# All expert weights resident in SBUF and read through registers, and scan runs of 128 steps, in a gated scan followed by a top-1 mixture of experts

## The chip, the core and the metric

The kernel runs on one core of a Trainium2 chip. The metric is the device time of one execution in microseconds (us), lower is better. Five engines work side by side on a core: PE (TensorE, matrix products; the profile counts its weight loads apart as PEld), DVE (VectorE), ACT (ScalarE), POOL (GpSimd) and SP (SyncE, which here issues most DMAs). Each engine has a sequencer that reads its instructions in order; register and address instructions run on the sequencer itself, and the profile marks these with a q (PEldq, SPq).

## The reference

A gated linear recurrence over time, and then for each token one expert of eight, chosen by a router.

```python
B, S, D = 4, 5056, 256            # x, r_gate, i_gate: (B, S, D)
N, E, F = 20224, 8, 1024          # w1: (E, D, F), w2: (E, F, D)
a_t = exp(8 * sigmoid(r_gate) * log(clip(sigmoid(a_param), 1e-6, 1 - 1e-6)))
xg = sqrt(max(1 - a_t * a_t, 1e-6)) * sigmoid(i_gate) * x
h = 0
for t in range(S):                # for each batch row and channel
    h = a_t[:, t] * h + xg[:, t]
    y[:, t] = h
x2 = y.reshape(N, D)
logits = x2 @ w_gate + modality_bias[modality_id]
e_idx = argmax(logits, axis=1)
gate = softmax(logits)[arange(N), e_idx]
for e in range(E):                # each token by its own expert only
    m = e_idx == e
    out[m] = gate[m, None] * (maximum(x2[m] @ w1[e], 0) @ w2[e])
```

All of it is float32. The kernel keeps that precision with numbers split in two fp16 parts (high and low): each product of the expert layers is three fp16 products, high by high, high by low and low by high.

## The kernel before

**The scan.** Time is cut into runs (`CHUNKS`): 19 runs of 256 steps, one of 128 and one of 64. A run takes all 4 batch rows, so 256 steps are 1024 tokens. `load_chunk` loads its three inputs by DMAs that SP issues (L467), `scan_chunk` makes the factors on ACT and DVE and scans on DVE (L518), `split_chunk` finds a scale (L606) and writes the two fp16 parts (L627 on ACT, L630 on DVE), `route_chunk` computes router and slot numbers, and `rows_part` turns the states into rows of tokens (DMA transposes, L669) and scatters them with POOL (L777) into a table `rows` in DRAM, which holds each expert's tokens in one place, in order of arrival. Every run costs the same number of small DVE instructions, whatever its length.

**The experts' weights.** The experts are put in an order by their router bias. Of each, w1 and w2 are loaded (1 MB each), scaled by a power of two, and split into two fp16 parts (`convert`). The parts of w2 stay in SBUF, in `w2f`. The parts of w1 are written to DRAM, into `w1s`.

**Pages.** The expert layers work on pages of 256 tokens (or 128; a few of 512, as two halves) of one expert. `choose_pages` picks, on DVE, the expert with the most tokens waiting; expert and place in the table are known only as numbers in a tile `sel`, so the program reads them into registers (`value_load`). For each page, SP (`page_weights`, L949 to L959) loads the w1 parts of the page's expert from `w1s` into one of three buffers `wt` (1 MB per page, L953), and `load_rows` the tokens, transposed, into `X` (L990).

**The expert layers** (`expert_layers`) are a pipeline on PE: layer 1 of a page in four quarters (L1065), each followed by a quarter of layer 2 of the page before (L1108). A quarter of layer 1 is 12 pairs of a weight load and a matmul: the stationary operand is a 128x128 block of w1, the streamed operand `X`, as many columns as the page has tokens. A quarter of layer 2 is 12 pairs for 256 tokens and 6 for 128: the stationary operand is a block of `H`, the streamed one 256 columns of w2. Layer 1's `wt` is a fixed address, since the page's weights were copied there. Layer 2 reads `w2f` at a place that depends on the page's expert, in a register:

```python
(wv[:, s, k, fs], cur.X[:, 2 * x + k, :])                              # layer 1: stationary, streamed
(prev.H[:, hx, f, rs_], w2f[:, ds(pg.ew + (f * 2 + wx) * D, D)])       # layer 2: stationary, streamed
```

The register is loaded once per page (L1088); each use of `ds(pg.ew + ...)` costs an address instruction on the sequencer of PE. Behind layer 1, ACT and DVE write the two parts of `H` (L1009, L1011); behind layer 2, ACT scales the output (L1020) and POOL scatters it (L1024).

**The order of the work** is fixed when the program is built: a planner (`run`) keeps a list of threads, each a generator that asks for an engine, a duration and a condition, and emits next the one that can start first. `START` lists the order of the first loads by hand. The first 28 pages may be "early": of an expert among those whose weights are ready, the first two experts at least, and of 128 tokens where fewer than 511 wait. The last pages are of 128 tokens; five of them stand in branches that run only where tokens are left, and none of the five ran in the profiled execution (PE read the register of 84 pages).

Of the kernel before, what the change touches and what calls it, by code (L numbers as in the profile page):

```python
# [9 lines left out]
F32 = mybir.dt.float32  # L10
F16 = mybir.dt.float16
# [17 lines left out]
CHUNKS = [(0, 256), (256, 256)] + [(512 + 256 * k, 256) for k in range(17)] + [(4864, 128), (4992, 64)]  # L29
BUFS = {  # L30
    "a": 3, "g": 2, "x": 2, "wt": 3, "H": 2, "X": 3, "ot": 3, "rt": 2, "sel": 4, "dg": 2,
# [5 lines left out]
TAIL_TAGS = "aaggxxa"  # L37
# [35 lines left out]
def kernel(  # L73
# [27 lines left out]
    w1s = dram.tile([E, P, 4 * FF], F16, name="w1s")  # L101

# [45 lines left out]
    for e in range(E):  # L148
        nc.gpsimd.memset(tieb8[:, e : e + 1], 0.125 * (E - 1 - e))
        nc.gpsimd.memset(kd[:, e : e + 1], float(E - 1 - e - 8 * e * NCAP))  # L150
    cpar = const.tile([P, 2], F32, name="cpar")
# [15 lines left out]
    nc.vector.tensor_reduce(out=top[:, :, 0], in_=mb[0:1], axis=AX.X, op=ALU.max)  # L167
    nc.vector.tensor_tensor(out=low, in0=mb[0:1], in1=top.broadcast_to([1, 2, E]), op=ALU.subtract)
# [21 lines left out]
    # half of 8 * log(clip(sigmoid(a_param)))  # L190
# [49 lines left out]
    def add(gen, prio, t=0.0, urgent=False):  # L240
        """prio: the lower the sooner, (on TensorE, on the other engines)"""
# [30 lines left out]
    WE = NF * 2 * D  # L272
    w2f = const.tile([P, E * WE + WE // 2], F16, name="w2f")
    w2r = w2f[:, 0 : E * WE].rearrange("p (e f s d) -> p e f s d", e=E, f=NF, s=2)

    def waiting(q):
        """where a matrix waits, as it came: from the middle of one place to that of the next"""
        return w2f[:, q * WE + WE // 2 : (q + 1) * WE + WE // 2].bitcast(F32)

    READY = "pages read the weights of experts that are ready"  # L280

    def weight_write(ins, q, what="w"):
        """a write of which the pages of before read nothing"""
        tc.declare_no_dep(ins, group=f"{what}_pages", reason=READY)
        tc.add_to_no_dep_group(f"{what}{q}", ins)

    def weight_read(ins, pg, what="w"):
        for q in range(pg.ready, E):
            tc.declare_no_dep(ins, group=f"{what}{q}", reason=READY)
# [13 lines left out]
    def scale_of(name, raw, sc, iv, factor):  # L303
        """sc: the power of two for a matrix, iv: what undoes it"""
        ss = sm.tile([P, 1], F32, name=f"ss{name}", tag="ss", bufs=16)
# [3 lines left out]
        pt = pso.tile([P, 512], F32, name=f"pt{name}", tag="po")  # L309
        # the upper halves of the words are the values as bf16: enough for a power of two  # L310
# [5 lines left out]
        jk = sm.tile([P, P], F32, name=f"jk{name}", tag="jk", bufs=1)  # L316
# [9 lines left out]
    ivc = const.tile([P, E], F32, name="ivc")  # L326

    def convert(k, name, raw, hi, lo, sc, q=None):
        """hi = sc * raw, rounded; lo = sc * raw - hi, by VectorE or by TensorE and ScalarE; a half at a time"""
        wrote = lambda ins: None if q is None else weight_write(ins.ins, q)  # L330
        if LO[k] == "P":
            yield "ACT", 0.2, room("dg")
            td = take("dg")
            dg = sm.tile([P, P], F32, name=f"dg{name}", tag="dg")
            nc.scalar.activation(dg, ident, AF.Copy, scale=sc)
        for v in range(2):
            fs = slice(4 * v, 4 * v + 4)
            if HI[k] == "A":
                yield "ACT", 1.0, None
                wrote(nc.scalar.activation(hi[:, fs, :], raw[:, fs, :], AF.Copy, scale=sc))  # L340
            else:
                yield "DVE", 0.63, None
                wrote(nc.vector.tensor_scalar(out=hi[:, fs, :], in0=raw[:, fs, :], scalar1=sc, scalar2=None, op0=ALU.mult))
            if LO[k] == "D":
                yield "DVE", 1.2, None
                wrote(nc.vector.scalar_tensor_tensor(
                    out=lo[:, fs, :], in0=raw[:, fs, :], scalar=sc, in1=hi[:, fs, :], op0=ALU.mult, op1=ALU.subtract
                ))
                continue
            for u in range(2):  # L350
                yield "PE", 1.25, room("ph"), 0.2
                tp = take("ph")
                us = slice(4 * v + 2 * u, 4 * v + 2 * u + 2)
                pl = psh.tile([P, 2, 256], F32, name=f"pl{name}_{v}{u}", tag="ph")
                nc.tensor.matmul(pl, dg, raw[:, us, :], start=True, stop=False)
                nc.tensor.matmul(pl, nid, hi[:, us, :], start=False, stop=True)
                yield "ACT", 0.48, None, -0.5
                wrote(nc.scalar.activation(lo[:, us, :], pl, AF.Copy))  # L358
                give("ph", tp)
        if LO[k] == "P":  # L360
            give("dg", td)

    # the loads before the expert layers start have a fixed order
    loads, seq = [], {"a": 0, "b": 0}
    for what in START.split():
        if what in seq:
            seq[what] += 1
            what += str(seq[what] - 1)
        loads.append(what)
    assert seq == {"a": E, "b": E}  # L370
    assert all(loads.index(f"a{e}") < loads.index(f"b{e}") for e in range(E // 2, E))
# [6 lines left out]
    def place(e):  # L378
        """the place in w2f where w1 waits"""
        return e + E // 2 if e < E // 2 else e  # L380

    def first_weights(e):
        """w1 of the e-th expert in the order, left in DRAM as its two parts"""
        tag = "wt"
        q = place(e)
        yield "DMA", 2.9, seen(("turn", loads.index(f"a{e}") - 1), *([("w1", e - E // 2)] if e >= E // 2 else [])), -9.0
        raw = waiting(q)
        o = nc.sync.value_load(order[0:1, e : e + 1], min_val=0, max_val=E - 1)
        weight_write(nc.sync.dma_start(
            raw.rearrange("p (k f) -> p k f", k=2), w1[ds(o, 1)].rearrange("o (k p) f -> p (o k) f", p=P)  # L390
        ).ins, q)
        went(f"a{e}")
        mark["got", 1, e] = plan["end"]
        yield "SP", 0.0, seen(("got", 1, e)), 0.0
        sc = sm.tile([P, 1], F32, name=f"sc1_{e}", tag="sc1", bufs=8)
        yield from scale_of(f"1_{e}", raw, sc, ivc[:, e : e + 1], 1.0)
        yield "SP", 0.0, room(tag), 0.0
        tw = take(tag)
        wt = pm.tile([P, 4 * FF], F16, name=f"wk{e}", tag=tag, bufs=BUFS[tag])
# [810 lines left out]
```

## Time and profile before

| what | value |
|---|---|
| time, median of 3 runs | 1205.32 us (1198.14 to 1214.27) |
| span of the profiled execution, first to last instruction | 1136.6 us |
| own time of the profiled execution | not given apart from its span; the median of the runs is 68.7 us above the span |
| PE busy | 949.4 us (84%) |
| DVE, ACT, POOL busy | 768.2 (68%), 588.2 (52%), 455.1 (40%) us |
| moved by DMA | 268.3 MB, 236 GB/s |
| mean granted clock of TensorE | 0.936 |

The span is what the profile can divide; what lies around it, 68.7 us, is taken as a constant. In the rows of the profile, "L1108" is line 1108 of the kernel, `po<-w2f,H` says what is written from what, and "x3840" is a count. A matmul's duration in the rows is from its start to its modelled end; matmuls overlap, so the pace of a row of them is told by the distance of their starts.

### The profile page before, as it was taken

The page shows a single profiled execution, that of the slowest core. Times are in us where ns is not written, and L with a number is a line of the kernel's source. Part 1 is how long each engine was busy: PE and PEld are TensorE (multiplying, and loading weights), DVE is VectorE, ACT ScalarE, POOL GpSimd, SP SyncE. Part 2 cuts the span into 40 slices and gives each one's busy share as a digit, 9 for nine tenths or more (in the row PEclk, how much of TensorE's full clock was granted, in tenths as well). Part 3 has the DMA queues.
Part 4 walks back from the last instruction along what each step waited for, and adds up shares of the span by engine and source line. Part 5 has one row for each costly group of instructions (what it writes and reads, how often), then busy time and mean ns, then how long its engine had stood idle before and what let it go on. Part 6 is the DMA issues. An engine that isn't in the chain of part 4 may idle for free.

```text
span 1136.6 us, 29582 instructions
## 1 busy us (share of the span) xinstructions
PE 949.4 (84%) x9139; PEld 818.5 (72%) x9139; DVE 768.2 (68%) x2544; ACT 588.2 (52%) x824; POOL 455.1 (40%) x496
## 2 busy tenths in 40 slices
PE   1423996898894998985999899999999999999993
PEld 1211875777783887874788678777778888889993
DVE  2896783778793978876787778687876433344561
ACT  4752752673743466666367566765754333333331
POOL 3026131615440626546544655375646311242121
PEclk9756998999996999998999999999999999999997
DMA  7799999999999999997999999999978635559999
GB/s 258 313 256 193 237 225 223 306 257 317 263 255 194 201 229 320 259 249 191 253 271 255 294 282 276 220 289 268 277 173 202 144 85 163 150 161 241 243 265 186
DMA packets 257752, 268.30 MB, mean 236 GB/s; under 512 B 216319, under 2 KB 224640, under 8 KB 237888
## 3 DMA queue, kind: packets, MB, share of 16 engines
q1 hardware_dynamic: 238848, 214.82, 77.6%
q0 software_dynamic: 15744, 42.92, 13.1%
q10 hardware_dynamic: 3008, 8.57, 2.3%
q8 instruction: 89, 1.46, 0.5%
q14 instruction: 63, 0.52, 0.2%
HBM read 172.62 MB, written 51.56 MB: 197 GB/s over the span
## 4 chain that ended last, share of the span: by engine, by line
PE 47%; DMA 20%; DVE 18%; issue 5%; SPq 4%; ACT 4%; POOL 1%; ACTq 0%; DVEq 0%; POOLq 0%
PE ph L1065 23%; PE po L1108 22%; DMA X<-rows 6%; DMA w2f<-in_moe_w_dram 6%; DVE g L518 4%; DVE H L1011 3%; DMA rows<-rt,di 2%; DVE mxy L606 2%; DVE g L504 1%; DMA iv<-iv 1%; SPq L669 1%; DVE a L630 1%; PE pt L314 1%; ACT H L1009 1%; DMA x<-in_x_dram 1%
## 5 line engine op out<-in xcount | busy, mean ns | idle before, releaser
L1065 PE MATMUL ph<-X,wt 128*128 128x256 f16 (+1 forms) x4224 | 491.8, 268 | 47.4 <-DMA X<-rows 46.0
L1108 PE MATMUL po<-w2f,H 128*128 x3840 | 486.9, 274 | 10.4 <-issue 7.4
L1065 PEld LDWEIGHTS <-wt 128*128 128x128 f16 x4224 | 390.2, 100 | 99.0 <-issue 51.0
L1108 PEld LDWEIGHTS <-H 128*128 128x128 f16 x3840 | 372.7, 98 | 61.8 <-issue 9.0
L1009 ACT ACTIVATE H<-ph 128x512 f16<-128x512 f32 (+1 forms) x352 | 195.1, 555 | 367.4 <-PE ph L1065 357.0
L1011 DVE SCALAR_TENSOR_TENSOR H<-ph,H 128x512 f16<-128x512 f32 (+1 forms) x352 | 222.1, 636 | 235.3 <-ACT H L1009 234.6
L1024 POOL DMA_INDIRECT out_dram<-ot,mt x160 | 200.1, 1251 | 405.9 <-ACT ot L1020 313.2
L777 POOL DMA_INDIRECT rows<-rt,di x158 | 213.3, 1350 | 246.2 <-DVE dmy L534 55.5
L1020 ACT ACTIVATE ot<-po,gt 128x256 f32<-128x256 f32 x160 | 75.4, 471 | 75.6 <-PE po L1108 69.2
L518 DVE TENSOR_TENSOR_SCAN g<-a,g 128x2048 f32<-128x2048 f32 (+2 forms) x21 | 87.5, 4168 | 0.6
L627 ACT ACTIVATE a<-g,scy 128x512 f16<-128x512 f32 (+2 forms) x84 | 53.5, 686 | 16.2 <-DVE scy L545 14.3
L630 DVE SCALAR_TENSOR_TENSOR a<-g,scy,a 128x512 f16<-128x512 f32 (+2 forms) x84 | 56.6, 711 | 0.2 <-ACT a L627 0.2
L314 PEld LDWEIGHTS <-w2f 128*128 128x128 bf16 x256 | 20.6, 118 | 43.7 <-DMA w2f<-in_moe_w_dram 42.1
L314 PE MATMUL pt<-w2f 128*128 128x128 bf16 x256 | 23.2, 259 | 33.2 <-DMA w2f<-in_moe_w_dram 32.7
L495 ACT ACTIVATE a<-a,ch 128x1024 f32<-128x1024 f32 (+2 forms) x42 | 48.9, 1186 | 3.3 <-DVE m1y L531 3.3
L504 DVE TENSOR_TENSOR g<-g,x 128x2048 f32<-128x2048 f32 (+2 forms) x21 | 45.4, 2160 | 7.7 <-ACT x L502 7.7
L486 ACT ACTIVATE g<-g 128x2048 f32<-128x2048 f32 (+2 forms) x21 | 38.0, 1808 | 17.8 <-DMA g<-in_i_gate_dram 17.7
L490 DVE SCALAR_TENSOR_TENSOR g<-g,x 128x2048 f32<-128x2048 f32 (+2 forms) x21 | 45.2, 2152 | 0.8 <-ACT g L486 0.6
L606 DVE TENSOR_REDUCE mxy<-g 128x4 bf16<-128x2048 f32 (+2 forms) x21 | 45.0, 2144 | 0.0
L498 ACT ACTIVATE x<-a 128x2048 f32<-128x2048 f32 (+2 forms) x21 | 38.0, 1809 | 3.0 <-issue 2.4
L502 ACT ACTIVATE x<-x 128x2048 f32<-128x2048 f32 (+2 forms) x21 | 38.0, 1809 | 0.4
L488 ACT ACTIVATE a<-a 128x2048 f32<-128x2048 f32 (+2 forms) x21 | 37.8, 1801 | 0.4 <-ACT wk L358 0.4
(161 smaller groups left out, 654.8 us busy)
## 6 DMA issues: line engine op xcount, KB each, us to landing
wt<-w1s SPq DMA_DIRECT2D x89, 1024.0 KB
a<-in_r_gate_dram SPq DMA_DIRECT2D x19, 1024.0 KB
g<-in_i_gate_dram SPq DMA_DIRECT2D x19, 1024.0 KB
x<-in_x_dram SPq DMA_DIRECT2D x19, 1024.0 KB
w2f<-in_moe_w_dram SPq DMA_DIRECT2D x16, 1024.0 KB
w1s<-wk ACTq DMA_DIRECT2D x8, 1024.0 KB
out_dram<-ot,mt POOLq DMA_INDIRECT x160
rows<-rt,di POOLq DMA_INDIRECT x158
```

What stands on the lines that cost most here:

```text
L314: nc.tensor.matmul(pt[:, 0:P], blk, blk, start=(j == 0), stop=(j == nb - 1))
L504: nc.vector.tensor_tensor(out=g, in0=g, in1=s, op=ALU.mult)
L518: nc.vector.tensor_tensor_scan(out=g, data0=a, data1=g, initial=0.0, op0=ALU.mult, op1=ALU.add)
L606: nc.vector.tensor_reduce(out=mx[:, 0:ng], in_=yg.rearrange("p h g t -> p g h t"), axis=AX.XY, op=ALU.max, apply_absolute_value=True)
L630: nc.vector.scalar_tensor_tensor(out=ys[:, 1, :, g, :], in0=yg[:, :, g, :], scalar=sc[:, g : g + 1], in1=ys[:, 0, :, g, :], op0=ALU.mult, ...
L777: ins = nc.gpsimd.indirect_dma_start(out=rows[:, :], out_offset=bass.IndirectOffsetOnAxis(ap=idx, axis=0), in_=src, in_offset=None, bounds ...
L1009: nc.scalar.activation(t.H[:, 0, hs, :], ph[:, :, 0:st], AF.Relu)
L1011: nc.vector.scalar_tensor_tensor(out=t.H[:, 1, hs, :], in0=ph[:, :, 0:st], scalar=0.0, in1=t.H[:, 0, hs, :], op0=ALU.max, op1=ALU.subtract,)
L1020: nc.scalar.activation(t.ot[:, a, :], po, AF.Copy, scale=t.gt[:, a : a + 1])
L1024: ins = nc.gpsimd.indirect_dma_start(out=out[:, :], out_offset=bass.IndirectOffsetOnAxis(ap=t.mt[:, a, 0:1], axis=0), in_=t.ot[:, a, :], i ...
L1065: nc.tensor.matmul(ph[:, v, 0:st], lhsT, rhs, start=(m == 0), stop=(m == len(mm) - 1))
L1108: ins = nc.tensor.matmul(po, lhsT, rhs, start=(f == 0 and m == 0), stop=(f == NF - 1 and m == len(mm) - 1))
```

## The change

- The split parts of w1 and w2 of all 8 experts stay in SBUF, in one tile `wall` (132 KB per partition). `w1s`, the buffers `wt` and the loads per page go away. `first_weights` and `second_weights` become one function, `weights`, and `page_weights` becomes `page_rows`, without the load of w1.
- Layer 1 takes its stationary blocks from `wall` at an address in a register. The register is loaded ahead of layer 1 (L1012) instead of layer 2.
- Runs of the scan: one of 64 steps and then 39 of 128. Rows go out in parts of 4 columns, not 8. The first loads (`START`) are run 0, run 1, four matrices, run 2, two matrices, and so on.
- The low parts of the weights are all made on DVE; before, four matrices went through PE and ACT. The output buffers hold 128 rows each, and the last pages' tokens lie in other buffers. Comments were taken out.

```diff
-CHUNKS = [(0, 256), (256, 256)] + [(512 + 256 * k, 256) for k in range(17)] + [(4864, 128), (4992, 64)]
+CHUNKS = [(0, 64)] + [(64 + 128 * k, 128) for k in range(39)]
...
-PART = 8
+PART = 4
...
-HI = "ADDADDADADAAADDD"
-LO = "PDDDDDDDDPPDPDDD"
-START = "0 a a a a 1 b 2 b 3 b a b 4 b 5 a b a b a b"
+HI = "ADADADADADADADAD"
+LO = "DDDDDDDDDDDDDDDD"
+START = "0 1 w w w w 2 w w 3 w w 4 w w 5 w w 6 w w w w"
...
-    WE = NF * 2 * D
-    w2f = const.tile([P, E * WE + WE // 2], F16, name="w2f")
+    WE = 4 * FF
+    wall = const.tile([P, 2 * E * WE + WE // 2], F16, name="wall")
...
-    def page_weights(pg):
+    def page_rows(pg):
...
-        yield "DMA", 2.9, allof(room(tag), seen(*[("w1s", e) for e in range(pg.ready)]))
+        yield "DMA", 0.1, seen(*[("e", e) for e in range(pg.ready)])
+        pg.off = nc.sync.value_load(pg.sel[0:1, 0:1], min_val=0, max_val=NULLS + 256 - pg.size)
...
-        pg.wt = (pm if tag == "wt" else pa).tile([P, 4 * FF], F16, name=f"wt{pg.n}", tag=tag, bufs=BUFS[tag])
-        weight_read(nc.sync.dma_start(pg.wt, w1s[ds(es, 1)].rearrange("o p f -> (o p) f")).ins, pg, "d")
...
+                        if pg.ew is None:
+                            pg.ew = nc.tensor.value_load(pg.sel[0:1, 2:3], min_val=0, max_val=(E - 1) * 2 * WE)
...
                         mm = [
-                            (wv[:, s, k, fs], cur.X[:, 2 * x + k, :])
+                            (wall[:, ds(pg.ew + (2 * k + s) * FF + f * P, P)], cur.X[:, 2 * x + k, :])
                             for k in range(2) for s, x in ((0, 0), (0, 1), (1, 0))
                         ]
...
-                            (prev.H[:, hx, f, rs_], w2f[:, ds(pg.ew + (f * 2 + wx) * D, D)])
+                            (prev.H[:, hx, f, rs_], wall[:, ds(pg.ew + WE + (f // 4 * 2 + wx) * FF + f % 4 * D, D)])
```

What the two programs hold, in the order in which an engine meets it (ISA is a register or address instruction; the names behind an instruction are what it writes and reads):

On PE, before the change, the end of a page's layer 1 and the first quarter of layer 2 of the page before:

```order
L1065 LDWEIGHTS wt_913
L1065 MATMUL ph_0_0_1039<-X_0_990,wt_913 128x256
L1088 TENSOR_LOAD sel_779
L1088 ISA x2
L1108 LDWEIGHTS H_0_934
L1108 ISA
L1108 MATMUL po_0_0_1080<-w2f,H_0_934 128x256
```

On PE after the change, at the same place of the first page:

```order
L1027 ISA
L1027 LDWEIGHTS wall
L1027 ISA
L1027 MATMUL ph_0_3_819<-X_0_725,wall 128x128
L1066 LDWEIGHTS H_0_761
L1066 ISA
L1066 MATMUL po_0_0_841<-wall,H_0_761 128x256
```

A pair of layer 1 had no address instruction and now has two, one ahead of the weight load and one ahead of the matmul; a pair of layer 2 has one, as before; the register's load stands ahead of layer 1 now. In the part that always runs there are 98 pages after the change (62 of 256 tokens, 36 of 128), where 84 ran before (68 with 72 tiles of 256 tokens, 16 of 128): with 512 tokens in a run, 19 of the 28 early pages are of 128 tokens, before none. That is 160 columns of 128 tokens in both.

On SP before the change, a page's instructions:

```order
L949 TENSOR_LOAD sel_828
L949 ISA x2
L953 ISA
L953 DMA wt_913<-w1s 128x4096
L954 TENSOR_LOAD sel_828
L990 ISA
L990 DMA_TRANSPOSE X_0_990<-rows 128x4x256
L991 DMA mt_0_991<-rows 128x2x2
```

And after:

```order
L914 TENSOR_LOAD sel_927
L914 ISA x2
L916 TENSOR_LOAD sel_927
L918 DMA pinv_1012<-iv_79 128x1
L950 ISA
L950 DMA_TRANSPOSE X_0_1036<-rows 128x4x256
L951 DMA mt_0_1037<-rows 128x2x2
```

The load of 1 MB ahead of the tokens is gone; the page's scale (`pinv`), which came later, stands ahead of them.

On SP at the start, before the change (run 0, four matrices w1, run 1, the first w2; the second w2 comes only behind run 2 and a run's transposes):

```order
L467 DMA a_238<-in_r_gate_dram 128x2048
L389 DMA w2f<-in_moe_w_dram 128x2x1024
L467 DMA a_382<-in_r_gate_dram 128x2048
L418 DMA w2f<-in_moe_w_dram 128x8x256
L669 DMA_TRANSPOSE rt_0_568<-a_238 128x8x128 x4
```

And after:

```order
L433 DMA a_236<-in_r_gate_dram 128x512
L433 DMA a_254<-in_r_gate_dram 128x1024
L390 DMA wall<-in_moe_w_dram 128x2x1024
L390 DMA wall<-in_moe_w_dram 128x8x256
L433 DMA a_413<-in_r_gate_dram 128x1024
L635 DMA_TRANSPOSE rt_0_477<-a_236 128x2x128 x4
```

Both matrices of the first two experts are now loaded behind 2.25 MB of run 0 and run 1, ahead of all else. (Rows that repeat, as the other inputs of a run and the second pair of matrices, are left out here.)

More of the change, by code (lines that the diff above doesn't have):

```diff
@@ L376, in went @@
             mark["turn", loads.index(what)] = plan["end"] - 4.0
[L378 to L387, printed above, removed]
-        o = nc.sync.value_load(order[0:1, e : e + 1], min_val=0, max_val=E - 1)
[L389 to L399, printed above, removed]
-        hi, lo = wt[:, 0 : 2 * FF], wt[:, 2 * FF :]
-        by8 = lambda t: t.rearrange("p (f d) -> p f d", f=NF)
-        yield from convert(e, f"1_{e}", by8(raw), by8(hi), by8(lo), sc)
-        mark["w1", e] = plan["end"]
-        yield "ACT", 0.1, None, 0.0
-        free["DMA"] = max(free["DMA"], plan["end"]) + 2.9
-        plan["end"] = free["DMA"] + 2.0
-        weight_write(nc.scalar.dma_start(w1s[e], wt).ins, e, "d")
-        give(tag, tw)
-        mark["w1s", e] = plan["end"]
@@ L822, in all_in @@
     def all_in():
-        return seen(*[("w", e) for e in range(E)])()
+        return seen(*[("e", e) for e in range(E)])()
     def enough():
@@ L877, in choose_pages @@
             if early:
-                pg.ready = next((e for e in range(2, E) if mark.get(("w", e), FAR) > plan["end"] + SLACK), E)
+                pg.ready = next((e for e in range(2, E) if mark.get(("e", e), FAR) > plan["end"] + SLACK), E)
             pages.append(pg)
@@ L1039, in expert_layers @@
             cur = None
-            if queue and queue[0].pg.n < count["turn"] and (prev is None or max(queue[0].ready, seen(("wt", queue[0].pg.n))()) < free["PE"] + WAIT):
+            if queue and queue[0].pg.n < count["turn"] and (prev is None or queue[0].ready < free["PE"] + WAIT):
                 cur = queue.pop(0)
@@ L1129 @@
     start_chunk(0)
-    for e in range(E):
-        for w, weights in enumerate((first_weights, second_weights)):
-            add(weights(e), (2, W_AT + W_STEP * (2 * e + w) if e > 1 else W_0 + 0.1 * (2 * e + w)))
+    for m in range(2 * E):
+        add(weights(m), (2, W_AT + W_STEP * m if m > 3 else W_0 + 0.1 * m))
     add(choose_pages(), (0, 4), urgent=True)
```

199 lines of the change are left out of this document (94 added, 105 removed).

## The prediction

> **What bounds the kernel now.** I read the page's busy shares, slices and chain first, then the groups by line, then single lines and short windows of PE, because the change edits PE's instruction stream. From the page:
>
> ```profile
> span 1136.6 us, 29582 instructions
> PE 949.4 (84%) x9139; PEld 818.5 (72%) x9139; DVE 768.2 (68%) x2544; ACT 588.2 (52%) x824; POOL 455.1 (40%) x496
> PE   1423996898894998985999899999999999999993
> PE 47%; DMA 20%; DVE 18%; issue 5%; SPq 4%; ACT 4%; POOL 1%; ACTq 0%; DVEq 0%; POOLq 0%
> ```
>
> PE is full from the third slice on and nearly without a hole in the last third. Its work is two groups, as two windows of the timeline and the lines themselves show (a line's row: count, then min/median/max in ns; PEldq is PE's sequencer):
>
> ```profile
> L1065 PEld LDWEIGHTS <-wt x4224: 95/98/181, 109.4 to 1115.1; 128*128 128x128 f16 x192
> L1065 PE MATMUL ph<-X,wt x4224: 219/272/421, 109.4 to 1115.1; 128*128 128x256 f16 x158, 128*128 128x128 f16 x34
> L1065 PEldq EVENT_SEMAPHORE  x82: 51/51/51, 109.3 to 1109.3; - x82
> L1108 PEldq FUSED_REGOPS  x3840: 42/46/51, 120.1 to 1118.3; - x192
> L1108 PE MATMUL po<-w2f,H x3840: 269/273/421, 120.5 to 1118.4; 128*128 x192
> 888.26 1.47 PE L1108 MATMUL po<-w2f,H 128*128 x12
> 889.57 1.47 PE L1065 MATMUL ph<-X,wt 128*128 128x256 f16 x12
> 516.89 3.10 PE L1108 MATMUL po<-w2f,H 128*128 x24
> ```
>
> Layer 2 (L1108) has one address instruction per matmul, 3840 of 46 ns; layer 1 (L1065) has none. A stretch of n matmuls lasts n-1 steps and one duration. At 888 us both layers step at (1.47 - 0.27)/11 = **0.109 us**: the array's pace for 256 columns. At 516.89, where 24 matmuls of layer 2 stand without layer 1 between them and nothing was queued ahead, they step at (3.10 - 0.27)/23 = **0.123 us**. So the sequencer needs 0.123 us for a pair with one address instruction, more than the array needs, and that is hidden today only because the 12 pairs of layer 1 between two quarters of layer 2 cost the sequencer little and let it run ahead again. How little, router matmuls bound from above, 32 pairs without an address instruction (chain of the end):
>
> ```profile
> 686.10 0.78 PE psl L644 x32
> ```
>
> 0.78/32 = 0.024 us a pair, in array and sequencer together.
>
> **Layer 1.** The change puts two address instructions into each pair of layer 1, the ones that had none. Nothing is left that lets the sequencer catch up, so PE moves at its sequencer's pace and the array's 0.109 no longer counts. The trace has no pair with two, so I bound it. From below: one pair of layer 2 plus the second instruction's own 46 ns, 0.123 + 0.046 = 0.169. From above: two pairs of layer 2, 0.246. Between: of 0.123, 0.046 is the instruction, 0.024 the pair itself, and 0.053 is left that comes with the instruction (fetching it, resolving the operand that needs it); twice 0.099 and once 0.024 are **0.222**. I take 0.222, nearer the upper end, because the sequencer shows such gaps wherever register instructions follow each other. At a page's register load:
>
> ```profile
> L1088 PEldq TENSOR_LOAD <-sel x1: 298/298/298, 675.5 to 675.5; - x1
> L1088 PEldq FUSED_REGOPS  x1: 151/151/151, 675.9 to 675.9; - x1
> L1088 PEldq SEQ_ASSERT  x1: 18/18/18, 676.1 to 676.1; - x1
> L1108 PEldq FUSED_REGOPS  x13: 42/46/46, 676.2 to 677.8; - x13
> ```
>
> From 675.5 to 676.2 are 0.7 us, of which the three instructions fill 0.467: 0.23 for three gaps, some 0.08 each.
>
> There are 62 pages of 256 tokens and 36 of 128, each 4 x 12 pairs of layer 1 whatever its size: 98 x 48 = 4704 pairs, 480 more than now. 4704 x 0.222 = **1044 us** (795 to 1157). Small pages, nearly as cheap per token on the array, become twice as dear per token:
>
> ```profile
> L1065 PE MATMUL ph<-X,wt 128*128 128x256 f16 x3456 | 438.5, 279 | 47.4 <-DMA X<-rows 46.0 <-DVE H L1011 1.4
> L1065 PE MATMUL ph<-X,wt 128*128 128x128 f16 x768 | 53.3, 219 | 0.0
> ```
>
> Now they take 438.5/3456 = 0.127 and 53.3/768 = 0.069; after, both 0.222.
>
> **Layer 2** keeps its 3840 pairs with one instruction each, now without cover: 3840 x 0.123 = **472 us**. **Register loads**, 0.7 us a page, were covered by what the sequencer had queued; the queue is empty now, so 98 x 0.7 = **69 us** count in full.
>
> [...]
>
> **The start.** Now the first layer 1 is at 109.44. Its chain runs over the second expert's w2, loaded late (chain, and timeline of PE):
>
> ```profile
> 65.10 12.58 DMA w2f<-in_moe_w_dram
> 99.74 19.32 DMA X<-rows
> 109.44 5.28 PE L1065 MATMUL ph<-X,wt 128*128 128x256 f16 x24 [17.82 <-DMA X<-rows]
> 0.00:119.00 119.00, 38.90 (x258) 25.39 (x258) 79.49 (x211) 59.43 (x58) 37.36 (x115) 0.73 0.92 251
> ```
>
> That load lands at 77.7, and 31.7 us of splitting, page choice and loads follow. After, 6.25 MB (6.55 million bytes) are asked for up to the fourth matrix; at the 251 GB/s of this stretch 26 us, with the wait for the order of the experts and shares of other loads some 38. 38 + 32 = **70 us** for the first layer 1, a gain of 39; I allow 55 to 95. The split on DVE alone has four matrices at about the cost of run 0, inside that.
>
> **The stages in between.** PE waited for the pages' tokens and for weights (waits of PE, 119 to 1118 us):
>
> ```profile
> PE ph L1065 <- DMA X<-rows: 28.2, 10, 8.9
> PE psl L528 <- DVE mxy L606: 21.2, 14, 2.3
> PE pt L314 <- DMA w2f<-in_moe_w_dram: 20.7, 5, 13.7
> ```
>
> 89 MB of page loads leave the DMA queues, and PE takes tokens more slowly, so most of this goes; I keep **20 us**. The shorter runs cost DVE more, but beside PE:
>
> ```profile
> L518 DVE TENSOR_TENSOR_SCAN g<-a,g 128x2048 f32<-128x2048 f32 x19 | 84.0, 4422 | 0.5
> L518 DVE TENSOR_TENSOR_SCAN g<-a,g 128x1024 f32<-128x1024 f32 x1 | 2.3, 2292 | 0.0
> L531 DVE TENSOR_REDUCE m1y<-psl 4x1 f32<-4x128 f32 x21 | 5.8, 277 | 1.7 <-PE psl L528 1.7
> ```
>
> A half run scans in 2.29 us against 4.42, so the large operations scale and add some 30 us; the two dozen small ones per run (0.28 and less) add about 5 us for each of 19 more runs, 95. DVE comes to some 900 us in a span far longer. If PE's cover were gone, these 125 us would show only as far as DVE became the bound. POOL scatters the same 318 columns. **The end:** the last matmuls stop at 1118.6, 18.0 before the span does; this stays.
>
> ```profile
> 1115.19 3.44 PE L1108 MATMUL po<-w2f,H 128*128 x30
> ```
>
> **Sum.** 70 + 1044 + 472 + 69 + 20 + 18 = 1693 us of span. The page gives the execution no time beside its span; the median of the runs is 68.7 above it: 1762 us, 46% over the 1205.3 of before.
>
> **The clock.** With PE waiting for addresses, the granted clock may fall. Stretches of before:
>
> ```profile
> 149.00:152.40 3.40, 2.12 (x13) 1.00 0.78 243
> 152.40:155.80 3.40, 2.00 (x24) 1.00 1.02 367
> 551.70:555.10 3.40, 1.18 (x9) 1.00 1.21 197
> 555.10:558.50 3.40, 3.40 (x18) 0.51 1.14 260
> ```
>
> After a stretch with 9 matmuls (9 x 0.109 = 0.98 of 3.40 us streaming, 29%) the clock was halved; after one with 13 (42%) it was not. Pages of 256 tokens will stream 2.62 of 12 x 0.222 + 12 x 0.123 = 4.14 us (63%): safe. Small pages stream 1.31 of 3.40 us (39%): between. At half clock layer 1 still fits in 0.222, and layer 2 goes from 0.123 to 0.218: at most 36 x 24 x 0.095 = 82 us, which I keep for the upper end. [...]
>
> **Rivals.**
>
> *The address instructions are hidden (faster).* If the sequencer prepared addresses during the array's waits and stayed ahead, layer 1 would step at 0.109 for 256 tokens. Then the start's gain of 39 and the 28.2 of waits for tokens count, against 20 more small pages x 48 x (0.069 - 0.064) = 5 us: 1205 - 39 - 28 + 5 = 1143 us. It decides as soon as two instructions and the pair fit in 0.109; one alone takes 0.123 at 516.89. For it speaks only that the same 0.123 is hidden today. Chance 0.05.
>
> *The second instruction is free.* Layer 1 then steps at 0.123: 4704 x 0.123 = 579 instead of 1044, 1762 - 465 = 1297 us. Chance 0.05, and 0.02 for a time between this rival and the first that lands within 2% of before.
>
> *Only its 46 ns count.* 795 instead of 1044: 1513 us. This also stands for a sequencer that is quicker when no profile is taken, of which the trace says nothing. Chance 0.15.
>
> *Layer 1 at 0.246 with a halved clock.* 1762 + 113 + 82 = 1957 us. Chance 0.08.
>
> That the change does not do what it says is hardly open: the order of instructions shows no load per page and two address instructions per pair.
>
> **How the numbers follow.** My forecast (layer 1 at 0.19 to 0.246, full clock) has 0.65: 1762 us. The range takes the third rival, what lies a little under it, and most of the fourth: 1450 to 1940, leaving out the two fast rivals (0.12) and the far end (some 0.06). Faster by over 2% is 0.05; within 2% (about what a measurement of this kernel can tell from no change) 0.02; slower 0.93.
>
> **What would show it.** In the profile after: address instructions at the line of layer 1, twice its 4704 matmuls; 12 matmuls of layer 1 stepping at about 0.22 us, for 128 and 256 tokens alike, and 12 of layer 2 at 0.123; PE idle before both lines put down to issue; the first layer 1 near 70 us; DVE near 900 us; the clock near 1 on large pages. I am wrong if layer 1 steps at 0.109 to 0.13, or if PE waits for DVE, ACT or tokens in the second half.

## The result, and the profile after

| what | before | after |
|---|---|---|
| time, median (lowest to highest) | 1205.0 us (1198.1 to 1214.3, 4 runs) | 1801.3 us (1797.8 to 1803.8, 4 runs) |
| ratio, 95% interval | 1 | 1.493 (1.485 to 1.502) |
| span of the profiled execution | 1136.6 us | 1799.5 us (its own time 1801.3) |
| PE, DVE busy | 949.4, 768.2 us | 1573.7, 882.7 us |
| moved by DMA | 268.3 MB, 236 GB/s | 167.4 MB, 93 GB/s |

The change makes the kernel 49% slower; 1762 us was forecast. The page of the changed kernel: span, busy times, the busy slices of PE with the granted clock, and the chain that ended last.

```profile
span 1799.5 us, 41612 instructions
PE 1573.7 (87%) x9666; PEld 908.8 (51%) x9666; DVE 882.7 (49%) x3466; ACT 685.5 (38%) x1093; POOL 422.9 (24%) x570
PE   2479799989993798999999999999999998999998
PEclk9978879988985799999999999999999999877878
PE 63%; issue 22%; DVE 6%; DMA 5%; POOL 2%; ACT 2%; SPq 1%; POOLq 0%; ACTq 0%; DVEq 0%; PEldq 0%
```

PE is the bound as before, but the second entry of the chain is now "issue" (22%, before 5%): time in which PE waited for nothing that the profile shows. The cause stands in the lines of layer 1 (L1027, once L1065) and layer 2 (L1066, once L1108); a row gives the count, then the duration as min/median/max in ns, then the first and last start in us:

```profile
L1027 PEldq FUSED_REGOPS  x9408: 2/46/1122, 71.7 to 1787.8; - x196
L1027 PE MATMUL ph<-X,wall x4704: 216/269/421, 72.3 to 1787.9; 128*128 128x256 f16 x124, 128*128 128x128 f16 x72
L1066 PEldq FUSED_REGOPS  x3840: 3/46/46, 83.0 to 1791.8; - x192
```

Layer 1 has 9408 address instructions, two for each of its 4704 matmuls. What they cost is told by PE's timeline and by the weight loads (PEld) in it: two stretches with 256 tokens and one with 128. A row gives start and length in us, what ran, how often, and in brackets the idle time before it with what ended it.

```profile
903.92 2.71 PE L1027 MATMUL ph<-X,wall 128*128 128x256 f16 x12
906.49 1.66 PE L1066 MATMUL po<-wall,H 128*128 x12
908.77 2.62 PE L1027 MATMUL ph<-X,wall 128*128 128x256 f16 x12 [0.62 <-issue]
904.50 0.93 PEld L1027 LDWEIGHTS <-wall 128*128 x5 [0.17 <-issue]
126.83 2.55 PE L1027 MATMUL ph<-X,wall 128*128 128x128 f16 x12
126.94 0.93 PEld L1027 LDWEIGHTS <-wall 128*128 x5 [0.20 <-issue]
```

Five weight loads in 0.93 us, of which the last lasts 0.096, are (0.93 - 0.096)/4 = **0.208 us** from start to start, with 256 and with 128 tokens alike. In the same trace the address instructions of layer 1 follow each other every 0.104 us (median), those ahead of a weight load and those ahead of a matmul alike. Layer 2's dozen steps at (1.66 - 0.27)/11 = 0.126. The array, which took 0.109 for a pair of either layer before (256 columns), waits for its sequencer in both.

### The profile page after: what moved, and what is told of

It reads as the page before. It is cut to its first block, busy times and chain, and to the rows that moved or that the text cites. A ratio compares the mean times of both kernels' runs of the same rounds, so it can differ in the third digit from the quotient of the medians.

```text
span 1799.5 us, 41612 instructions
## 1 busy us (share of the span) xinstructions
PE 1573.7 (87%) x9666; PEld 908.8 (51%) x9666; DVE 882.7 (49%) x3466; ACT 685.5 (38%) x1093; POOL 422.9 (24%) x570
## 4 chain that ended last, share of the span: by engine, by line
PE 63%; issue 22%; DVE 6%; DMA 5%; POOL 2%; ACT 2%; SPq 1%; POOLq 0%; ACTq 0%; DVEq 0%; PEldq 0%
PE ph L1027 41%; PE po L1066 21%; DMA wall<-in_moe_w_dram 2%; POOL out_dram L984 2%; DMA X<-rows 1%; DVE a L596 1%; DVE wall L350 1%; DMA x<-in_x_dram 1%; PE psl L610 1%; ACT H L969 1%; DVE H L971 1%; POOL rows L743 1%; PE pt L317 0%; SPq L635 0%; DVE g L484 0%
## 5 line engine op out<-in xcount | busy, mean ns | idle before, releaser
L1027 PE MATMUL ph<-X,wall 128*128 128x256 f16 (+1 forms) x4704 | 989.0, 264 | 113.4 <-issue 34.8
L1027 PEld LDWEIGHTS <-wall 128*128 x4704 | 458.2, 99 | 620.9 <-issue 153.8
L1066 PE MATMUL po<-wall,H 128*128 x3840 | 587.7, 289 | 2.0 <-issue 1.1
L1066 PEld LDWEIGHTS <-H 128*128 128x128 f16 x3840 | 386.9, 102 | 134.4 <-issue 10.8
L484 DVE TENSOR_TENSOR_SCAN g<-a,g 128x1024 f32<-128x1024 f32 (+1 forms) x40 | 90.6, 2265 | 1.4
L593 ACT ACTIVATE a<-g,scy 128x256 f16<-128x256 f32 (+1 forms) x160 | 69.6, 494 | 1.7 <-DVE scy L511 0.9
L596 DVE SCALAR_TENSOR_TENSOR a<-g,scy,a 128x256 f16<-128x256 f32 (+1 forms) x160 | 68.8, 471 | 0.8 <-ACT a L593 0.8
L461 ACT ACTIVATE a<-a,ch 128x512 f32<-128x512 f32 (+1 forms) x80 | 61.9, 800 | 2.9 <-DVE mk L865 1.4
L470 DVE TENSOR_TENSOR g<-g,x 128x1024 f32<-128x1024 f32 (+1 forms) x40 | 48.1, 1202 | 9.8 <-ACT x L468 7.7
L456 DVE SCALAR_TENSOR_TENSOR g<-g,x 128x1024 f32<-128x1024 f32 (+1 forms) x40 | 48.0, 1200 | 1.7 <-DMA x<-in_x_dram 1.4
L572 DVE TENSOR_REDUCE mxy<-g 128x4 bf16<-128x1024 f32 (+1 forms) x40 | 47.8, 1196 | 0.0
L468 ACT ACTIVATE x<-x 128x1024 f32<-128x1024 f32 (+1 forms) x40 | 41.8, 1046 | 14.8 <-DVE x L466 14.5
```

What stands on the lines that cost most here:

```text
L461: nc.scalar.activation(sl, sl, AF.Exp, scale=ch[:, h : h + 1], bias=ch[:, h : h + 1])
L468: nc.scalar.activation(s, s, AF.Sqrt, scale=-0.25)
L484: nc.vector.tensor_tensor_scan(out=g, data0=a, data1=g, initial=0.0, op0=ALU.mult, op1=ALU.add)
L593: nc.scalar.activation(ys[:, 0, :, g, :], yg[:, :, g, :], AF.Copy, scale=sc[:, g : g + 1])
L596: nc.vector.scalar_tensor_tensor(out=ys[:, 1, :, g, :], in0=yg[:, :, g, :], scalar=sc[:, g : g + 1], in1=ys[:, 0, :, g, :], op0=ALU.mult, ...
L1027: ins = nc.tensor.matmul(ph[:, v, 0:st], lhsT, rhs, start=(m == 0), stop=(m == len(mm) - 1))
```

## The experiments

The kernels of one set ran on the same chip, beside the kernel before. Its median was 1147.7 us in the first set (b_again, a_static1, a_xreg, b_reg1), 1207.6 in the second (a_again, a_early256, b_runs, b_start1) and 1200.3 in the third (b_noload, a_static12, b_runs_2, b_short2). So ratios are compared across sets, not times.

### The kernel before, again (b_again)

> The kernel before, unchanged, to learn what its time holds beside its span. The prediction took 68.7 us around the span as a constant, but the kernel after spends 1.8 us there (1801.3 against 1799.5). Theory A: a run's time is its span plus about 2 us for this kernel too, and the profiled execution of before (1136.6 us) was simply a faster execution than those that gave 1205; then each run here shows a span within 5 us of its time, and spans differ by tens of us between executions. Rival: 60 to 70 us lie around the span of this kernel in every run.

Measured: 1143.3 us, ratio 0.9996 (0.994 to 1.005). The profiled run took 1134.35 us, its span is 1132.6: 1.75 us lie around the span, as 1.8 do in the changed kernel. The "68.7 us around the span" of the prediction don't exist. By that the profiled execution of before, with its span of 1136.6, took about 1138 us, like those of this set; the times that stood beside it (1198 to 1214) are of slower executions.

### Layer 1 at a fixed address (a_static1)

```diff
-(wall[:, ds(pg.ew + (2 * k + s) * FF + f * P, P)], cur.X[:, 2 * x + k, :])
+(wall[:, (2 * k + s) * FF + f * P : (2 * k + s) * FF + f * P + P], cur.X[:, 2 * x + k, :])
```

> The kernel after, but layer 1 reads the first expert's w1 at a fixed address for every page, so its pairs have no address instruction; the output is then another expert's. Everything else is as after: 98 pages, short runs, resident weights. Theory (PE's sequencer, 0.208 us for a pair with two address instructions): layer 1 returns to the array's pace and lets the sequencer run ahead; 62 pages x 10.5 us + 36 x 5.3 us = 841 us, with some 60 of other matmuls, 72 for the start and 70 to 150 of waits: 1040 to 1150 us. Rival 1 (short runs, small pages or waits for tokens set the time): above 1500 us. Rival 2 (the 0.208 is not the address instructions but the reading of weights from the one large tile): no change, 1800.

Measured: 1149.0 us, ratio 1.006 (1.002 to 1.011). Here layer 1 reads the w1 of one expert for all pages. Page and timeline of this kernel:

```profile
PE 951.5 (83%) x9666; PEld 831.8 (73%) x9666; DVE 869.7 (76%) x3466; ACT 673.1 (59%) x1093; POOL 443.2 (39%) x570
904.77 1.47 PE L1027 MATMUL ph<-X,wall 128*128 128x256 f16 x12
906.08 1.47 PE L1066 MATMUL po<-wall,H 128*128 x12
```

PE is back at 951.5 us, and both layers step at (1.47 - 0.27)/11 = 0.109. The whole slowdown hangs on layer 1's address instructions. The rest of the change (no reload, short runs, earlier start) comes to about nothing in sum (0.2 to 1.1% slower); why is asked below.

### One address instruction instead of two (a_xreg)

```diff
+zr = nc.tensor.value_load(zt, min_val=0, max_val=16)           # a register that holds 0
-(wall[:, ds(pg.ew + (2 * k + s) * FF + f * P, P)], cur.X[:, 2 * x + k, :])
+(wall[:, (2 * k + s) * FF + f * P : ...], cur.XR[:, ds(zr + (2 * x + k) * st, st)])
```

> The kernel after, with layer 1's weights at a fixed address (so another expert's output) and its streamed operand X at an address in a register that holds zero: one address instruction per pair in both layers. Theory (cost per instruction): layer 1 steps at 0.124 us like layer 2, for 128 and 256 tokens alike; 4704 x 0.124 + 3840 x 0.124 + 69 for page loads + 72 start + 100 to 150 of waits and hiccups: 1300 to 1370 us. Rival 1 (cost per pair once any address is in a register): 0.208, 1800 us. Rival 2 (a register on the weight load is what costs, on the streamed operand it is nearly free): below 1200 us.

Measured: 1376.2 us, ratio 1.207 (1.190 to 1.224), just above the range that was expected. The streamed operand has the register now, and that costs one instruction a pair:

```profile
L1029 PEldq FUSED_REGOPS  x4704: 42/46/56, 68.0 to 1362.7; - x196
904.23 0.59 PEld L1029 LDWEIGHTS <-wall 128*128 128x128 f16 x5
```

(0.59 - 0.096)/4 = 0.124 us a pair in layer 1, the same as layer 2. So a pair of layer 1 steps at the array's 0.109 without an address instruction (a_static1), at 0.124 with one and at 0.208 with two. The second instruction adds 0.084 us, neither its own 46 ns nor nothing; 4704 x 0.084 = 395 us. The times, 1801 and 1376 us, are of different chips, but the two traces agree with it: from start to next start layer 1 takes 986.5 us in the changed kernel and 614.0 here, 372 less.

### The kernel before with a register in its address (b_reg1)

```diff
-(wv[:, s, k, fs], cur.X[:, 2 * x + k, :])
+(pg.wt[:, ds(zr + (2 * s + k) * FF + f * P, P)], cur.X[:, 2 * x + k, :])
```

> The kernel before with one thing changed: layer 1 reads the page's copied weights at an address that a register holding zero is added to. Weights are still reloaded per page, runs and pages are as before. Theory: two address instructions per pair of layer 1 (4224 x 0.208 = 879), layer 2 without cover (476), 84 register loads x 0.7 = 59, start 109, waits and hiccups 60 to 130, end 18: 1600 to 1680 us. Rival (the slowdown of the change comes with the resident weights, the short runs or the small pages): about 1205 us.

Measured: 1620.7 us, ratio 1.421 (1.399 to 1.444), inside the range. Nothing else differs from before: reload, long runs and 88 tiles as they were (one of 48 blocks per tile keeps its fixed address).

```profile
L1068 PEldq FUSED_REGOPS  x8272: 3/46/3083, 91.7 to 1611.7; - x197
904.05 0.72 PEld L1068 LDWEIGHTS <-wt 128*128 x4
```

(0.72 - 0.096)/3 = 0.208. The form of the address alone makes the slowdown, wherever the weights lie. The price is that of a register as stationary operand: two instructions a pair. One instruction was measured on the streamed operand alone; a single one ahead of the weight load was not run.

### The changed kernel again (a_again)

> The changed kernel as it is, beside the kernel before, which took 1148 us in the runs of the other experiments and 1205 us beside the first runs of the change. Theory A: the changed kernel goes at the pace of PE's sequencer nearly throughout, and that does not follow what made the kernel before 57 us shorter; 1785 to 1810 us, as first measured, and a ratio near 1.56. Rival B: whatever makes the kernel before shorter makes every kernel shorter by 5%; 1715 us. In the profile under A: layer 1 steps at 0.208 us a pair, layer 2 at 0.124.

Measured: 1800.9 us, on a chip where the kernel before took 1207.6; ratio 1.501 (1.462 to 1.540). The time is the one of theory A, but the run doesn't tell the theories apart: the kernel before took 1205 us beside the first runs of the change and 1208 here, so the changed kernel was never run where the kernel before takes 1148. Whether what moves the kernel before by 5% from set to set moves one that follows its sequencer is not shown.

### Fewer small pages (a_early256)

```diff
-size = next(z for z in (256, P) if left >= 2 * z - 1)
+size = 256
```

(and a page is chosen early only where 511 tokens have come.)

> The changed kernel with early pages of 256 tokens only: 72 pages of 256 and 16 of 128, so 88 instead of 98, for the same tokens. Theory A: a page costs PE's sequencer 48 x 0.208 us of layer 1 and 0.7 us of register load, 10.7 us, whatever its size; ten pages less are 107 us less: 1694 us (1670 to 1725, some of it given back where the first pages have to wait for more tokens). Rival B: the cost goes by tokens, or the waits of the first 700 us decide: 1780 to 1810 us. The granted clock, which fell on small pages, stays near 1 for longer under both.

Measured: 1674.2 us, ratio 1.395 (1.359 to 1.432); 127 us less than the changed kernel beside it, where 107 were worked out. The cost goes by pages, not by tokens. The clock was higher as well (0.940 against 0.912 in the mean); how much of the further 20 us it made was not separated. The same stretch of this kernel (first row) and of the changed one (second); columns are length, busy time of PE, PEld, DVE, ACT and POOL (with counts), granted clock, DMA share and GB/s:

```profile
72.00:300.00 228.00, 190.01 (x1287) 115.03 (x1288) 157.49 (x557) 99.86 (x148) 65.61 (x74) 0.95 0.56 140
```

```profile
72.00:300.00 228.00, 192.94 (x1224) 117.77 (x1224) 134.16 (x514) 80.42 (x128) 51.06 (x54) 0.82 0.51 122
```

In this stretch the clock was 0.82 with small early pages and 0.95 without them.

### Runs and reload: where did the rest of the change go?

Four kernels ask for the price of short runs and of the reload, each without the other.

**b_runs**, and once more in the third set, **b_runs_2**: the kernel before with the changed kernel's runs.

```diff
-CHUNKS = [(0, 256), (256, 256)] + [(512 + 256 * k, 256) for k in range(17)] + [(4864, 128), (4992, 64)]
+CHUNKS = [(0, 64)] + [(64 + 128 * k, 128) for k in range(39)]
```

> The kernel before with the changed kernel's runs of the scan (64 steps, then 39 of 128) and nothing else changed: reload per page, parts of 8 columns and the order of the first loads as before; 34 pages of 128 tokens and 63 of 256. Theory A (runs cost DVE about 100 us more, beside PE, and the earlier first page is lost again): 1145 to 1175 us against 1148. Rival B: DVE or the loads of twenty more pages become the bound of the first half: 1180 to 1230 us. Rival C: the earlier start counts in full: 1110 to 1130 us. DVE busy near 880 us under all.

> The kernel before with the changed kernel's runs of the scan, again, beside its counterparts without the reload. It came to 1.113 times the kernel before where 1.00 to 1.02 was the expectation. Theory A: short runs and the reload together crowd the DMA queues, so tokens and weights come late; 1.09 to 1.13 again, while the changed kernel with fixed addresses, which has the short runs without the reload, stays near 1.00. Rival B: the conditions of that one set of runs did it: 1.00 to 1.04.

Measured: 1337.7 us, ratio 1.113 (1.094 to 1.132), and again 1335.3 us, 1.123 (1.108 to 1.139). None of the theories for b_runs went so high; the second time it fell in the range of theory A, which had been drawn from the first.

**b_noload**: the kernel before, its load per page cut from 4096 to 64 columns, layer 1 at a fixed address in `w2f`.

```diff
-nc.sync.dma_start(pg.wt, w1s[ds(es, 1)].rearrange("o p f -> (o p) f"))
+nc.sync.dma_start(pg.wt[:, 0:64], w1s[ds(es, 1)].rearrange("o p f -> (o p) f")[:, 0:64])
-(wv[:, s, k, fs], cur.X[:, 2 * x + k, :])
+(w2f[:, (2 * k + s) * FF + f * P : (2 * k + s) * FF + f * P + P], cur.X[:, 2 * x + k, :])
```

> The kernel before without its reload: a page still issues its load, but of 16 KB instead of 1 MB, and layer 1 reads the split w1 at a fixed address of the place of the first expert, with no address instruction. Long runs and pages as before. Left out of the computation: each page's own w1. With the kernel before, the runs of the scan changed alone, and the changed kernel with fixed addresses, it fills a table of two edits: runs long or short, reload or none. Theory A: the reload is worth something only where short runs crowd the DMA queues; with long runs PE's waits for tokens (33 us) shrink by half: ratio 0.97 to 0.995 to the kernel before. Rival B: all waits for loads of the first 600 us go, 33 for tokens and 33 for weights: 0.93 to 0.96. Rival C: nothing, 0.995 to 1.01.

Measured: 1145.8 us, ratio 0.962 (0.950 to 0.974), between theories A and B; its interval reaches into both.

**a_static12**: a_static1 with layer 2 at a fixed address as well.

```diff
-wall[:, ds(pg.ew + WE + (f // 4 * 2 + wx) * FF + f % 4 * D, D)]
+wall[:, WE + (f // 4 * 2 + wx) * FF + f % 4 * D : WE + (f // 4 * 2 + wx) * FF + f % 4 * D + D]
```

> The changed kernel with fixed addresses in both expert layers, so that PE has no address instruction at all (the register is still loaded once per page). Left out of the computation: each page's own expert. Theory A: the one address instruction of layer 2 is hidden as long as layer 1 has none, so this equals the kernel with layer 1 alone fixed, 1.00 to 1.015 of the kernel before. Rival B: it costs something there too: 0.95 to 0.985.

Measured: 1191.3 us, ratio 0.997 (0.993 to 1.001), just under theory A's range; a_static1 had 1.006 (1.002 to 1.011). What layer 2's own instruction costs beside a layer 1 without any is about a per cent by these two ratios, which are of different sets; by their intervals it is under 2%.

The third set has all four corners, without address instructions in layer 1, as ratios to the kernel before:

| kernel | long runs | short runs |
|---|---|---|
| reload per page | 1 | 1.123 |
| no reload | 0.962 | 0.997 |

(The kernel of the last corner also has the changed kernel's order of first loads and of rows, and layer 2 at a fixed address.) In parts of the time of the kernel before, doing without the reload is worth 4% with long runs and 13% with short ones, and short runs cost 12% with the reload and 3 to 4% without: in sum nothing, as a_static1 showed. What the two do to each other is seen in PE's waits of b_runs, b_noload and a_static12, the costliest for tokens and for the scan (us in all, number of waits, the longest in us):

```profile
PE ph L1065 <- DMA X<-rows: 87.8, 32, 10.0
PE psl L528 <- DVE mxy L606: 59.4, 18, 10.8
```

```profile
PE psl L528 <- DVE mxy L606: 37.5, 14, 10.3
PE ph L1065 <- DMA X<-rows: 14.8, 3, 5.9
```

```profile
PE ph L1027 <- DMA X<-rows: 46.3, 13, 6.7
PE psl L494 <- DVE mxy L572: 27.1, 18, 5.2
```

With short runs and the reload, PE waited 87.8 us for tokens, in 32 places; with neither 14.8 in 3; the kernel before, with the reload alone, 33.2 in 9 (b_again). That these waits make the whole 12% is not shown: the clock fell as well (0.884 in b_runs, 0.939 in b_noload), and short runs bring more pages, so that b_runs has 97 tiles and moves 282 MB where the kernel before has 88 and 268.

### Is the earlier start worth something by itself? (b_start1, b_short2)

```diff
-START = "0 a a a a 1 b 2 b 3 b a b 4 b 5 a b a b a b"
+START = "0 a b a b 1 a a 2 b 3 b a 4 b 5 a b a b a b"
```

> The kernel before with only the order of its first loads changed: both matrices of the first two experts right behind run 0 (a b a b, then run 1), ahead of the w1 of the third and fourth. Theory A (the second expert's w2 holds back the first layer 1, which now starts at about 105 us; what comes before it is lost for good): layer 1 starts near 75 to 85 us and the time falls by 15 to 30 us, 1118 to 1135 against 1148. Rival B: PE then waits for tokens and weights until the scan has caught up, as in the changed kernel with fixed addresses, where a lead of 35 us was gone by the middle: 1140 to 1155 us.

Measured: 1214.9 us, ratio 1.008 (1.003 to 1.014). The edit didn't do what theory A needed. The load of the second expert's w2 and the first layer 1, of b_again and of this kernel:

```profile
65.43 0.41 SPq L418 DMA_DIRECT2D w2f<-in_moe_w_dram  x1
100.25 3.96 PE L1065 MATMUL ph<-X,wt 128*128 128x256 f16 x20 [7.78 <-DMA X<-rows]
```

```profile
20.52 0.37 SPq L418 DMA_DIRECT2D w2f<-in_moe_w_dram  x1
100.56 2.72 PE L1065 MATMUL ph<-X,wt 128*128 128x256 f16 x12 [5.25 <-DMA X<-rows]
```

The load was brought forward by 45 us and layer 1 was not: in both kernels it starts behind its tokens. So that load is not what holds the first layer 1 back. b_short2 cuts the first 256 steps into two runs of 128 instead.

```diff
-CHUNKS = [(0, 256), (256, 256)] + [(512 + 256 * k, 256) for k in range(17)] + [(4864, 128), (4992, 64)]
+CHUNKS = [(0, 128), (128, 128)] + [(256 + 256 * k, 256) for k in range(18)] + [(4864, 128), (4992, 64)]
```

> The kernel before with only the first 256 steps cut into two runs of 128, the rest shifted by 256 steps (22 runs in all). It asks if the earlier start can be had without forty short runs. Theory A: layer 1 starts 10 to 20 us earlier (near 85 us), and with long runs behind it the lead is kept in part: ratio 0.98 to 0.995. Rival B: the lead is lost while PE waits for tokens in the next 200 us, as with the changed order of the first loads: 1.00 to 1.02. 26 pages of 128 tokens instead of 16 cost the array 10 x 48 x 0.014 = 7 us under both.

Measured: 1254.8 us, ratio 1.054 (1.042 to 1.065), worse than either theory. The first layer 1 came 24 us earlier, and the time grew by 5%:

```profile
76.54 3.78 PE L1065 MATMUL ph<-X,wt 128*128 128x256 f16 x17 [4.49 <-DMA X<-rows]
PE ph L1065 <- DMA X<-rows: 49.9, 6, 16.0
```

A start that is early by itself gains nothing here: PE waits later, up to 16.0 us at a time, for tokens. Why ten more small tiles and one more run lose 5% is open. No version that was run and does the whole computation beats the kernel before.

## Why the prediction was right, point by point

The forecast was 1762 us, by a sum of 1693 us of span and 68.7 around it. The time is 1801, the span 1799.5. The mechanism of the slowdown is as said: two address instructions a pair, and PE at its sequencer's pace. That the sum comes within 2.2% is luck: the span alone is 106 us short, since waits, clock and small matmuls were sized too low and layer 1 too high, and a term that doesn't exist makes up for most of it. (One reading of the page was off: PE's slices are full from the fifth on, not from the third. No term rests on it.)

**Layer 1** was sized at 0.222 us a pair, 1044 us. The steady step is 0.208: 4704 x 0.208 = 978 us, 66 less. The guess of "twice 0.099 and once 0.024" put too much on the instruction; of what the 0.053 beside its 46 ns is made, no run shows. Measured are 0.104 for each of the two instructions, with the weight load and the matmul inside that time. Whole dozens are slower: (2.71 - 0.27)/11 = 0.222 and (2.62 - 0.27)/11 = 0.214, for hiccups such as the idle 0.17 us in the row at 904.50; with the quicker step from a dozen of layer 1 to layer 2, a pair takes 0.210 over the whole trace (986.5 us). The second rival took the second address instruction to be free. It is not: a pair takes 0.109 us with none (a_static1), 0.124 with one (a_xreg) and 0.208 with two.

**Layer 2** was 472 us at 0.123. The median distance of its matmuls' starts in the trace is 0.124: 3840 x 0.124 = 476.

**Register loads** were 69 us. A page's load leaves PE idle as forecast; the row at 908.77 shows 0.62 us before a layer 1, put down to issue. That is the median of the 98 pages too: some 60 us.

**The start** was 70 us (55 to 95); the first layer 1 is at 72.28:

```profile
72.28 2.80 PE L1027 MATMUL ph<-X,wall 128*128 128x128 f16 x13 [1.29 <-DMA X<-rows]
```

The number holds, but the path behind it doesn't, so this too was luck. The prediction had the second expert's w2 hold back the first layer 1; b_start1 brought that load forward and the start stayed. With the old order of loads and the short runs (b_runs) it comes sooner still:

```profile
65.39 3.07 PE L1065 MATMUL ph<-X,wt 128*128 128x128 f16 x36 [0.17 <-DMA X<-rows]
```

So it is the shorter first run, whose tokens are ready sooner, that brings the start forward. That it is a gain was implied by the sum; in b_short2 and a_static1 (first layer 1 at 69.83) the earlier start made no shorter time.

**The waits** were the step that failed in size: 20 us. The terms with their measured sizes, 72 + 978 + 476 + 60 + 7 (the end, below), are 1593 us, so 206 of the span are left. Idle time of PE between the first layer 1 and the last layer 2, and the worst stretch:

```profile
72.30:1792.70 1720.40, 1556.02 (x9522) 894.01 (x9521) 838.54 (x3301) 648.52 (x1047) 409.05 (x472) 0.90 0.36 90
500.00:700.00 200.00, 148.99 (x946) 85.75 (x947) 119.15 (x409) 97.49 (x148) 62.06 (x81) 0.80 0.45 127
PE psl L494 <- DVE k L856: 8.4, 1, 8.4
PE psl L708 <- DVE oh L697: 8.1, 3, 4.4
```

1720.4 - 1556.0 = 164 us are idle. By the matmul that comes next in the trace, 75 of them lie ahead of a layer 1 for which a register is loaded (60 are the loads themselves), 50 ahead of small matmuls of the scan and the router, and 36 inside layer 1's stretches, put down to issue: these are such hiccups, in which PE waited for nothing that the profile shows. So waits are some 15 + 50 = 65 us, where 20 were kept. 51 of the idle time lie between 500 and 700 us. The two rows are the longest waits for DVE there. The first is put down to `k`, but its matmul reads the maxima `mxy`, whose reduction ended at 577.96, 0.05 us ahead of it: it waited for the scan. The second is for the router's slots (`oh`). The prediction showed a row for the scan and sized the waits by tokens and weights. From 900 us on, no wait is longer than 1.2 us and most are put down to issue, as forecast.

PE's own small matmuls between the pages were left out of the sum as well: 9522 - 8544 = 978, at 0.024 us some 23. Steps of layer 2 at half the clock (next) make 39. The other 79, the 36 of hiccups among them, are not split here.

**The clock** did fall on small pages, a case that the prediction kept for the upper end:

```profile
1600.00:1780.00 180.00, 169.76 (x914) 96.33 (x914) 39.01 (x253) 25.69 (x64) 12.70 (x13) 0.78 0.11 22
1707.09 1.44 PE L1066 MATMUL po<-wall,H 128*128 x6
1710.39 0.92 PE L1066 MATMUL po<-wall,H 128*128 x6
```

Over the last pages, all of 128 tokens, it was 0.78. At any time the trace has it either full or half (55 stretches at 1.0 and 55 at 0.5); 0.78 is a mean. Layer 2 steps at (1.44 - 0.42)/5 = 0.204 in one stretch, at half clock (0.50 from 1707.1 to 1708.5), where a matmul lasts 0.42 us, and at (0.92 - 0.27)/5 = 0.130 in another, at 1.00. In the whole trace, 453 of 3482 steps inside layer 2's stretches began at half clock, with a median of 0.213 (forecast 0.218); that is 39 us more than at 0.124, where up to 82 were kept. PE was busy in 170 of these 180 us and never idle for more than 0.7 us at a time. What sets the fall is not shown: the prediction placed small pages between a stretch of 9 and one of 13 matmuls of the kernel before, by its own estimate, and in another of its stretches with 13 (783.80 to 787.20, clock 1.00) the clock was halved right behind it as well (0.51 from 787.20 to 790.60). Large pages kept 0.99:

```profile
700.00:1000.00 300.00, 286.63 (x1825) 163.67 (x1825) 172.52 (x623) 146.96 (x222) 90.85 (x105) 0.99 0.42 110
```

**The end** was 18 us ("this stays") and is 7. In the kernel before (b_again's timeline), whose last matmul ended at 1114.3, SP still issued loads for the last pages, which did not run:

```profile
1116.68 3.38 SPq L990 DMA_TRANSPOSE tail<-rows  x1
1122.55 2.01 SPq L990 DMA_TRANSPOSE tail<-rows  x1
```

The last matmul of the changed kernel is at 1792.6 of 1799.5; its SP had issued the last of its own at 1776, with no reload among them. That the reload is what held SP up before was not tested.

**Around the span** was the other wrong step: 68.7 us, measured 1.8. It was a difference between executions, read as a part of each. It covered most of the 106 us that the span lacked: luck.

**DVE** was to be near 900 us, beside PE: 882.7, 49% of the span.

Of the rivals, the hidden instructions (1143 us) and the free second one (1297) are refuted by the step of 0.208; "only its 46 ns" would have been 0.169; 0.246 with a halved clock was too dear in layer 1 and half right on the clock.

## What to carry to other kernels

Before an operand gets an address in a register, count the address instructions per matmul and find out what covers them: one per pair in layer 2, beside a layer 1 with none, cost about a per cent, two per pair in layer 1 set the pace (0.208 us against the array's 0.109), and a reload by DMA beside PE's work was the cheaper way to the same data (1205 us against 1801). Price the parts of a change alone: here no reload was worth 4 to 13%, by the length of the runs, and short runs took it back. Check the path behind a term too: the start came out at 72 us for another reason than the one that was given. Take the time around a span from one execution that has both, not from a span of one and the median of others.

## What the runs showed of the hardware that was not expected

- A register as the address of the stationary operand costs two address instructions a pair (9408 for 4704), as that of the streamed operand one (4704 for 4704). A pair lasts 0.208 and 0.124 us, though each instruction is recorded with 46 ns; those of layer 1 in the changed kernel follow each other every 0.104 us.
- The clock fell to half in parts of a stretch where PE was busy 94% of the time and idle for at most 0.7 us at a time (0.78 in the mean over 180 us).
- The kernel before took 1148 us on one chip and 1200 to 1208 on two others; the changed one took 1801 both times, beside a kernel before that took 1205 and 1208. Where the kernel before loses these 55 us is open.
